# Seven block products instead of eight in the first half of the odd batches, and a new order of the sums they need

## The chip, the cores and the metric

The kernel runs on one core of a Trainium2 chip. The metric is the device time of one execution in microseconds (us), as a median over runs. All arithmetic of the matrix products is in 32-bit floats. The engines are TensorE (PE, with its weight loads shown as PEld), the vector engine (DVE), ScalarE (ACT), GpSimd (POOL) and SyncE (SP, which issues DMAs).

## The reference

A cross attention between 512 tokens and 32 state rows for each of 8 batches and 8 heads, and behind it a two-layer block with the activation h · cos(h). Cut to what matters:

```python
# x: (8, 8, 512, 64), state: (8, 8, 32, 64)
scores  = softmax(scale * x @ state.T)       # 512 x 32 for each head
xread   = scores @ state                     # 512 x 64
scores2 = softmax(scale * state @ x.T)
sread   = scores2 @ x                        # 32 x 64
rows = concatenate([xread, sread])           # 544 rows for each batch, 512 wide over the heads
h = rows @ w_in                              # 512 -> 2048, the first layer
g = h * cos(h)
out = g @ w_out                              # 2048 -> 512, the second layer
```

## The kernel before

**Stages.** Batch b has 16 tiles f of 128 hidden columns for its 512 tokens; the state rows of all batches are 16 more tiles at the end. The loop at the bottom takes one tile a step, 144 steps, and s is the step within a batch. It emits all engines' instructions in the order in which each engine is to run them: nothing reorders them later, and each engine runs its own list in order.

**The first layer.** The attention's second product is folded into the first layer: `sw` is the state times `w_in` (`products`, `products_kept`), `aT` the normalised attention weights, and h = sw · aT with an inner dimension of 256, in two pieces of 128. A plain tile (`hidden`) is two products of 128 x 128 weights with 512 columns, each of which shows as two instructions in the profile (a 32-bit product is made in two parts).

**Strassen's products.** `seven(t)` names the tiles whose first layer is made otherwise: two neighbouring tiles, t and t2, are a 2 x 2 block matrix (weights b11, b12, b21, b22) times the two halves of the tokens, and are made with seven products of 256 columns in place of eight. Before, these are the tiles of batches 2, 4 and 6 (`t.phase` is b % 2 * 2 + f // 8, so phases 0 and 1 are an even batch, 2 and 3 the two halves of an odd one). This needs:

- `halves(b)`: four differences of halves of aT into `aS`, on the vector engine, once a batch. For an even batch it stands five steps ahead. For a batch that follows a `seven` batch it would stand at s = 14; before, that place was never reached.
- `sw_sums(t)`: t1, t2, t4 in `swS` and a new b21 in place, four 128 x 128 operations for each pair, on Pool. For the first pair of an even batch it is emitted three steps ahead (just before `gate4`), for all others two steps ahead, at the end of the step, behind `blocks`.
- `hidden_a`: four of the products, one step ahead of the pair, into two PSUM tiles; a ScalarE copy; and `sums_a`, three additions on the vector engine.
- `hidden_b`: the other three products in the pair's own first step; `sums_b`, two additions. The tile pool of h has two PSUM tiles, and `hidden_a` and `hidden_b` take both, so each needs the sums of the other done.

**The activation.** `gate` (ScalarE, a rounding), `gate2` (vector, a difference), `gate3` (ScalarE, the sine) and `gate4` (vector, the product with h) make g = h · cos(h) in a slot of `g_all`. For a plain tile h is read in PSUM; for a `seven` tile it lies in `g_all` already.

**The second layer** uses seven block products too, over a pair of batches (`Pair`, `sums`, `sums2`, `p7`, `p4`, `output`). It needs differences of the tiles of both batches: `minus`, which runs on the vector engine when `soon` is true and the pair isn't the first, else on Pool. In phase 2 this is b0 = t - b0 for each tile; in phase 3 there are three. `output` multiplies a tile three steps after it was made (`LAG`). In phases 0 to 2 it also emits up to one left-over product of the pair before. `blocks` makes sums of blocks of w_out on Pool, at steps 16 to 22, 32 and 33.

**Order within a step** (the loop): `hidden_b` with its sums (and `halves` at s = 14), or `hidden`; `hidden_a` for the next pair; `gate`, `gate2`, `sums_a`, parts of the next batch's attention, `gate3`, one deferred store, the early `sw_sums`, `gate4`, `sums`, more parts, `halves`, `blocks`, the late `sw_sums`, `sums2`, and last `output` of the tile three steps back. Step 29 is tile 13 of batch 1, step 32 the first tile of batch 2.

Of the kernel before, what the change touches and what calls it, by code (L numbers as in the profile page):

```python
# [21 lines left out]
def kernel(  # L22
# [8 lines left out]
    nc = tc.nc  # L31
# [151 lines left out]
    def fetch(n):  # L183
        nonlocal n_fetched
        while n_fetched < n:
            dst, src = loads[n_fetched]
            if f64:
                m, w = dst.shape[1:]

                at_, c0 = (n_fetched - 2) % 3, 0  # L190
                if n_fetched < 4:
                    at_, c0 = n_fetched // 2, n_fetched % 2 * 2 * m * w
                if n_fetched >= N_LOADS:
                    at_ = 3 + n_fetched - N_LOADS
                raw = raw_at[at_].bitcast(I32)[:, c0:c0 + 2 * m * w]
                raw = raw.rearrange("p (m f) -> p m f", m=m)
                nc.sync.dma_start(out=raw, in_=src.bitcast(I32))
                raws[n_fetched] = raw.rearrange("p m (f w) -> p m f w", w=2)
            else:
                nc.sync.dma_start(out=dst, in_=src)  # L200
            n_fetched += 1
# [49 lines left out]
    class Attention:  # L251
# [126 lines left out]
        def sums(self):  # L378
            self.reduce1([self.z1[:, j] for j in range(2)], ALU.add)
            self.inverse(self.m1 if self.b == 0 else self.i12)  # L380
# [72 lines left out]
    def part(b, name, *args):  # L453

        if b not in attn:
            attn[b] = Attention(b)
        getattr(attn[b], name)(*args)
        if (name, args) == ("reads", (1,)) and b + 1 < B:
            if b > 0:
                attn[b + 1] = Attention(b + 1)  # L460
                attn[b + 1].load_tokens()
            load_x(b + 1)
# [5 lines left out]
    def hidden(t):  # L468
        t.hp = hps.tile([P, S], F32, name="h")[:, 0:t.n]
        for i in range(t.kn):  # L470
            nc.tensor.matmul(out=t.hp, lhsT=t.lhs(i), rhs=t.rhs(i),  # L471
                             start=(i == 0), stop=(i == t.kn - 1))
# [4 lines left out]


    def seven(t):
        return t.pair is not None and t.b > 1 and t.phase < 2  # L480

    def new_pair(t):
        return t.b % 2 == 0 and t.f == 0
# [9 lines left out]
    def blocks_of(t):  # L495
        sw = sw_of[t.b, P * t.f // WC]
        c = P * t.f % WC
        return [sw[:, j, c + P * r:c + P * r + P] for r in range(2)
                for j in range(2)]

    def sw_sums(t):
        b11, b12, b21, b22 = blocks_of(t)
        t1, t2, t4 = [swS[:, i] for i in range(3)]
        sub = ALU.subtract
        for o, x1, x2, op in ((t1, b21, b22, ALU.add), (t2, t1, b11, sub),
                              (t4, b12, t2, sub), (b21, b11, b21, sub)):
            nc.gpsimd.tensor_tensor(o, x1, x2, op=op)  # L507

    LO, HI = slice(0, HS), slice(HS, S)

# [36 lines left out]
    def hidden_b(t):  # L547
        b11, b12, b21, b22 = blocks_of(t)
        t.h1, t.h2 = [hps.tile([P, S], F32, name="h") for _ in range(2)]
        product_of(t.h1[:, LO], b12, aT_of[t.b][:, 1, LO])  # L550
        product_of(t.h2[:, HI], swS[:, 2], aT_of[t.b][:, 1, HI])
        product_of(t.h2[:, LO], b22, aS[:, 3])
# [29 lines left out]
    def minus(pr, out, a, b, soon=False):  # L582
        engine = nc.vector if soon and pr.n else nc.gpsimd
        engine.tensor_tensor(out, a, b, op=ALU.subtract)  # L584
# [78 lines left out]
    def sums(t):  # L663
        pr, i = t.pair, t.i
        pr.b[t.phase, i] = t
        if t.phase == 2:
            minus(pr, pr.b[0, i].g, t.g, pr.b[0, i].g, True)
        if t.phase == 3:
            minus(pr, pr.b[0, i].g, t.g, pr.b[0, i].g, True)
            minus(pr, pr.b[2, i].g, t.g, pr.b[2, i].g)  # L670
# [99 lines left out]
    def tiles():  # L770
        pr = None
        for b in range(B):
            if b % 2 == 0:
                pr = Pair(b // 2, pr)
            for f in range(NF):
                t = Tile()
                t.b, t.f, t.pair = b, f, pr
                t.phase, t.i = b % 2 * 2 + f // NH, f % NH
                t.n, t.kn = S, 2
                c = slice(P * f % WC, P * f % WC + P)  # L780
                t.lhs = lambda i, b=b, nt=P * f // WC, c=c: (
                    sw_of[b, nt][:, i, c])
                t.rhs = lambda i, b=b: aT_of[b][:, i]
                yield t
        for n in range(NF):
            t = Tile()
            t.b, t.n_th, t.f = B, n, (n + NH) % NF
            t.pair, t.last_pair, t.phase = None, pr, None
            t.n, t.kn = B * Ns, NK
            cols = slice(P * t.f, P * t.f + P)  # L790
            t.lhs = lambda i, cols=cols: w_in[:, i, cols]
            t.rhs = lambda i: sT[:, :, Ns * i:Ns * i + Ns]
            yield t


    def warm(n, to):

        for _ in range(n):
            nc.tensor.matmul(out=to, lhsT=zeros[:, 0:P], rhs=zeros, start=True,  # L799
                             stop=True)  # L800
# [123 lines left out]
    all_tiles = list(tiles())  # L924
    for step, t in enumerate(all_tiles):
        s = step % NF
        if s == 0 and t.b < B:
            steps = plan(t.b)
        todo = [p[s] if t.b < B else [] for p in steps]

        def go(n):
            for p in todo[n]:
                part(*p)

        last, conv = conv_at.get(step - 1, -1), conv_at.get(step, -1)
        if step == B * NF + (0 if f64 else 8):
            fetch(N_LOADS + 2)
        if step == 4:
            warm(1, acc[MAIN][0])
        ahead = all_tiles[step + 1:step + 3]  # L940
        if seven(t):
            if t.f % 2 == 0:
                hidden_b(t)
                sums_b(t)
                if s == NF - 2 and seven(all_tiles[step + 2]):
                    halves(t.b + 1)
        elif step != 1:
            hidden(t)
        first = len(ahead) > 1 and seven(ahead[0]) and ahead[0].f % 2 == 0
        if first:  # L950
            if not seven(t):

                h = t.hp
                take_slot(t)
                nc.scalar.copy(t.g, h)
            hidden_a(*ahead)
        if step == 0:
            hidden(all_tiles[1])
            warm(3, acc[MAIN][0])
            gate(t)  # L960
            gate2(t)
            convert(3, "bcdf")
            convert(4, "1")
            go(0)
        else:
            go(0)
            if step == 5:
                states(1, acc[SIDE][1])
            if not (seven(t) and t.f % 2):
                gate(t)  # L970
            gate2(t)
            if step == 3:
                warm(4, acc[MAIN][0])
                part(0, "products", 1, SIDE)
            if first:
                sums_a(ahead[0])
            go(1)
            go(3)
            if step == 1:
                convert(4, "bcdf")  # L980
            elif last >= 0:
                convert(last, "bcdf")
            if conv >= 0 and not todo[1]:
                convert(conv, "1")
        gate3(t)
        if seven(t) and t.f % 2 == 0:
            gate(t.second)
        if step == 3:
            part(0, "products_kept", 1, SIDE)
        if later:  # L990
            later.pop(0)()
        for u in all_tiles[step + 3:step + 4]:
            if seven(u) and new_pair(u):
                sw_sums(u)
        gate4(t)
        if conv >= 0 and todo[1] and step > 0:
            convert(conv, "1")
        if t.pair is not None:
            sums(t)
        if step == 6:  # L1000
            states_kept(1, acc[SIDE][1])
        go(2)
        if conv >= 0:
            convert(conv, "2")
        go(4)
        for u in all_tiles[step + 5:step + 6]:
            if seven(u) and new_pair(u):
                halves(u.b)
        if step in block_at:
            blocks(*block_at[step])  # L1010
        for u in all_tiles[step + 2:step + 3]:
            if seven(u) and u.f % 2 == 0 and not new_pair(u):
                sw_sums(u)
        if t.pair is not None:
            sums2(t)
        while len(line) >= (LAG if step >= 2 * NH else LAG + 1):
            output(line.pop(0))
        line.append(t)
# [32 lines left out]
```

## Time and profile before

| what | value |
|---|---|
| median of 5 runs | 769.31 us (768.81 to 770.35) |
| the profiled execution | 769.34 us, of which the span from first to last instruction is 767.5 us |
| granted TensorE clock | 1.000 |
| second layer, L622, 128x512 | 896 instructions, 413.6 us busy, 598 ns each |
| first layer, plain, L471, 128x512 | 320 instructions, 150.8 us busy, 594 ns each |
| first layer, seven products, L512, 128x256 | 336 instructions, 100.9 us busy, about 380 ns each |
| subtractions of tiles, L584 | 80 on Pool (1435 ns), 48 on the vector engine (697 ns) |
| block sums, L507 | 96 on Pool, 453 to 985 ns |
| DMA | 43.52 MB, 57 GB/s over the span |

How to read it: TensorE's instructions overlap, so the sum of their busy times is more than the time that they take; their spacing is read from the starts in the timeline. A row of a timeline has the start and the duration in us, the engine, the line of the kernel, the operation, the tile written and the tiles read, their shapes, how many such instructions follow each other, and in brackets the idle time ahead of it with what ended it. Short waits of TensorE behind a start can hide in the modelled end of the instruction before.

### The profile page before, as it was taken

Reading aid. Unit: us, or ns where it says so; the run is one execution under the profiler, and the core shown is the slowest. Engines: PE = TensorE matmul, PEld = TensorE weight load, DVE = VectorE, ACT = ScalarE, POOL = GpSimd, SP = SyncE. Lnnn points to the kernel's source line nnn. Section 1 sums busy time; section 2 is a strip of 40 time slices with the busy share of each in tenths; the row PEclk is TensorE's granted clock in tenths of the full one; section 3 lists DMA queues with packets and bytes.
Section 4 is the critical chain, followed back from the end, with each engine's and each line's share of the span. In section 5 each row is a group of like instructions: output and inputs, shape, how many; then the busy total and the mean of one; then the engine's idle time right before and its main releaser. Section 6 shows DMA issues by size and latency. Waiting matters only on the chain.

```text
span 767.5 us, 8094 instructions
## 1 busy us (share of the span) xinstructions
PE 755.7 (98%) x2808; PEld 366.9 (48%) x2808; DVE 487.3 (63%) x786; ACT 314.1 (41%) x511; POOL 227.8 (30%) x214
## 2 busy tenths in 40 slices
PE   8998999999999999999999999999999999999997
PEld 4443443444555434445555434455554444455554
DVE  5778787836896558847886558748876546432431
ACT  3877944532254325333362335333443333212112
POOL 2344278876120000653220001751210006500200
PEclk9999999999999999999999999999999999999999
DMA  9596471050002510340105211420100115000021
GB/s 246 168 273 198 137 104 28 8 102 1 12 16 47 91 28 2 54 83 0 29 0 100 39 27 16 76 46 0 28 1 14 23 20 138 0 1 14 15 41 41
DMA packets 161960, 43.52 MB, mean 57 GB/s; under 512 B 153920, under 2 KB 153920, under 8 KB 161920
## 3 DMA queue, kind: packets, MB, share of 16 engines
q1 hardware_dynamic: 161024, 42.49, 25.8%
q10 hardware_dynamic: 768, 0.39, 0.2%
q8 instruction: 22, 0.36, 0.2%
q0 software_dynamic: 128, 0.13, 0.1%
q14 instruction: 18, 0.15, 0.1%
HBM read 34.08 MB, written 8.91 MB: 56 GB/s over the span
## 4 chain that ended last, share of the span: by engine, by line
PE 91%; DVE 3%; POOL 2%; ACT 2%; DMA 1%; issue 1%; SPq 0%; DVEq 0%; POOLq 0%; ACTq 0%
PE o L622 49%; PE h L471 20%; PE h L512 9%; PE at L319 4%; PE o L742 4%; PE at L409 2%; PE o L319 1%; POOL g_all L584 1%; PE at L392 1%; DMA g_all<-in_moe_w_in_dram 1%; POOL w_out L910 0%; DVE q L568 0%; ACT q L565 0%; PE o L799 0%; DMA s<-in_state_dram 0%
## 5 line engine op out<-in xcount | busy, mean ns | idle before, releaser
L622 PE MATMUL o<-g_all,w_out 128*128 128x512 f32 x512 | 236.3, 598 | 0.4 <-POOL w_out L242 0.4
L584 POOL TENSOR_TENSOR g_all<-g_all 128x512 f32<-128x512 f32 x80 | 112.9, 1435 | 240.4 <-DVE g_all L578 240.4
L622 PE MATMUL o<-g_all,s 128*128 128x512 f32 x384 | 177.3, 598 | 0.0
L471 PE MATMUL h<-aT,sw 128*128 128x512 f32 x320 | 150.8, 594 | 2.9 <-DVE g_all L578 2.4
L568 DVE TENSOR_TENSOR q<-q,h 128x512 f32<-128x512 int32 (+1 forms) x93 | 59.4, 638 | 147.6 <-ACT q L565 147.6
L622 PEld LDWEIGHTS o<-g_all,w_out 128*128 128x128 f32 x512 | 93.8, 190 | 118.4 <-issue 114.6
L571 ACT ACTIVATE q<-q,halfpi 128x512 f32<-128x512 f32 (+1 forms) x144 | 100.9, 701 | 87.6 <-DVE q L568 87.5
L565 ACT ACTIVATE q<-h 128x512 int32<-128x512 f32 (+1 forms) x93 | 52.2, 562 | 201.1 <-PE h L471 200.9
L622 PEld LDWEIGHTS o<-g_all,s 128*128 128x128 f32 x384 | 70.8, 190 | 88.6 <-issue 86.6
L471 PEld LDWEIGHTS h<-aT,sw 128*128 128x128 f32 x320 | 60.1, 190 | 79.9 <-issue 66.5
L578 DVE TENSOR_TENSOR g_all<-h,q 128x512 f32<-128x512 f32 (+1 forms) x93 | 59.2, 637 | 35.0 <-ACT q L571 34.6
L565 ACT ACTIVATE q<-g_all 128x512 int32<-128x512 f32 x51 | 31.8, 623 | 90.9 <-DVE g_all L558 90.5
L568 DVE TENSOR_TENSOR q<-q,g_all 128x512 f32<-128x512 int32 x51 | 36.5, 716 | 28.6 <-ACT q L565 28.6
L242 POOL TENSOR_TENSOR w_out<-w_out,s 128x1024 int32<-128x1024 int32 x10 | 23.9, 2393 | 77.6 <-DVE w_out L237 62.8
L578 DVE TENSOR_TENSOR g_all<-g_all,q 128x512 f32<-128x512 f32 x51 | 37.0, 726 | 10.5 <-ACT q L571 10.4
L507 POOL TENSOR_TENSOR swS<-sw 128x128 f32<-128x128 f32 x24 | 11.4, 476 | 84.0 <-PE h L512 66.1
L584 DVE TENSOR_TENSOR g_all<-g_all 128x512 f32<-128x512 f32 x48 | 33.5, 697 | 1.6
L445 ACT COPY sw<-at 128x512 f32<-128x512 f32 x50 | 26.7, 586 | 10.4 <-PE at L319 10.0
L242 POOL TENSOR_TENSOR w_in<-w_in,s 128x1024 int32<-128x1024 int32 (+1 forms) x10 | 19.3, 1931 | 37.3 <-DVE w_in L237 22.0
L471 PE MATMUL h<-st_all,w_in 128*128 128x256 f32 x128 | 30.2, 379 | 0.0
L512 PE MATMUL h<-aS,swS 128*128 128x256 f32 x96 | 28.7, 380 | 1.0 <-POOL swS L507 1.0
L742 PE MATMUL o<-w_out,g_all 128*128 128x512 f32 x64 | 29.6, 592 | 0.0
(103 smaller groups left out, 788.2 us busy)
## 6 DMA issues: line engine op xcount, KB each, us to landing
out_dram<-ot SPq DMA_DIRECT2D x132, 64.0 KB, 2.0
g_all<-in_moe_w_out_dram SPq DMA_DIRECT2D x8, 1024.0 KB, 5.1
g_all<-in_moe_w_in_dram SPq DMA_DIRECT2D x6, 1024.0 KB, 5.3
xT<-in_x_dram SPq DMA_DIRECT2D x96, 64.0 KB, 2.5
x_b<-in_x_dram SPq DMA_DIRECT2D x24, 256.0 KB, 4.6
x_b<-in_x_dram SPq DMA_DIRECT2D x16, 128.0 KB, 4.2
g_all<-in_moe_w_in_dram SPq DMA_DIRECT2D x4, 512.0 KB, 6.2
x_b<-in_moe_w_out_dram SPq DMA_DIRECT2D x1, 1024.0 KB, 5.9
```

Of the source, the lines that this page charges most:

```text
L242: nc.gpsimd.tensor_tensor(bits, bits, e, op=ALU.add)
L319: nc.tensor.matmul(out=(to or at)[j][Ns * k:Ns * k + Ns, 0:n], lhsT=w[D * j:D * j + D, self.b, Ns * k:Ns * k + Ns], rhs=r(slice(D * j, D * ...
L445: (copy or nc.scalar.copy)(sw_of[self.b, nt][:, j, c0:c1], to[j][:, 0:c1 - c0])
L471: nc.tensor.matmul(out=t.hp, lhsT=t.lhs(i), rhs=t.rhs(i), start=(i == 0), stop=(i == t.kn - 1))
L512: nc.tensor.matmul(out=out, lhsT=w, rhs=r, start=True, stop=True)
L565: nc.scalar.activation(t.q.bitcast(I32), t.hp, func=ACTF.Copy, bias=0.25)
L568: nc.vector.tensor_tensor(t.q, t.q.bitcast(I32), t.hp, op=ALU.subtract)
L571: nc.scalar.activation(t.q, t.q, func=ACTF.Sin, bias=halfpi, scale=-TWO_PI)
L578: nc.vector.tensor_tensor(t.g, t.hp, t.q, op=ALU.mult)
L584: engine.tensor_tensor(out, a, b, op=ALU.subtract)
L622: nc.tensor.matmul(out=acc[bank][ch], lhsT=w[:, i, P * ch:P * ch + P], rhs=g.g, start=(i == 0), stop=(i == NH - 1))
L742: nc.tensor.matmul(out=acc[MAIN][i], lhsT=t.g[:, P * i:P * i + P], rhs=w_out[:, :, t.f, :], start=(t.n_th == 0), stop=(t.n_th == NF - 1))
```

## The change

Four edits:

1. `seven` covers phase 2 as well: tiles 0 to 7 of batches 3, 5 and 7. With it the branch at s = 14 of batches 2, 4 and 6 runs `halves` for the odd batch that follows.
2. `sw_sums` chooses its engine: the vector engine for the first pair of batch 2, Pool for all others.
3. The subtraction b0 = t - b0 of phase 2 goes from the vector engine to Pool in all pairs of batches (in the first pair it was there already).
4. The call of `sw_sums` two steps ahead moves from the end of the step, behind `blocks`, to just before `gate4`, where the three-steps-ahead call stood; both are now one loop.

```diff
     def seven(t):
-        return t.pair is not None and t.b > 1 and t.phase < 2
+        return t.pair is not None and t.b > 1 and t.phase < 3
...
         sub = ALU.subtract
+
+        engine = nc.vector if t.b < 2 or t.b == 2 and t.f == 0 else nc.gpsimd
         for o, x1, x2, op in ((t1, b21, b22, ALU.add), (t2, t1, b11, sub),
                               (t4, b12, t2, sub), (b21, b11, b21, sub)):
-            nc.gpsimd.tensor_tensor(o, x1, x2, op=op)
+            engine.tensor_tensor(o, x1, x2, op=op)
...
         if t.phase == 2:
-            minus(pr, pr.b[0, i].g, t.g, pr.b[0, i].g, True)
+            minus(pr, pr.b[0, i].g, t.g, pr.b[0, i].g)
...
-        for u in all_tiles[step + 3:step + 4]:
-            if seven(u) and new_pair(u):
+        for u, new in zip(all_tiles[step + 2:step + 4], (False, True)):
+            if seven(u) and u.f % 2 == 0 and new_pair(u) == new:
                 sw_sums(u)
         gate4(t)
...
         if step in block_at:
             blocks(*block_at[step])
-        for u in all_tiles[step + 2:step + 3]:
-            if seven(u) and u.f % 2 == 0 and not new_pair(u):
-                sw_sums(u)
```

## The prediction

> **What bounds the kernel now.** I read the page's busy line first, then busy time by window for the first halves of the batches, then the timeline of TensorE, and last those of Pool and the vector engine where TensorE stood still.
>
> ```profile
> PE 755.7 (98%) x2808; PEld 366.9 (48%) x2808; DVE 487.3 (63%) x786; ACT 314.1 (41%) x511; POOL 227.8 (30%) x214
> ```
>
> A busy TensorE could still be a slow one, so the windows come next: first half of batch 3 (plain products), then all of batch 4 (seven products).
>
> ```profile
> 254.60:296.00 41.40, 41.40 (x138) 17.13 (x137) 25.46 (x39) 12.38 (x21) 0.00 (x0) 1.00 0.20 32
> 338.10:422.30 84.20, 84.20 (x352) 45.97 (x351) 62.53 (x108) 34.98 (x61) 18.68 (x31) 1.00 0.17 30
> ```
>
> Columns: window, its length, then busy time and instructions of TensorE, weight loads, vector engine, ScalarE, Pool; then the granted clock. TensorE is busy for the whole of both windows at clock 1.00. In batch 3's first half Pool does nothing and the vector engine works 25.46 of 41.40 us, 61%; in batch 4 it works 62.53 of 84.20, 74%, and TensorE still doesn't wait. So the order of TensorE's own instructions sets the time, and an instruction taken from it is worth its spacing.
>
> Those spacings are in TensorE's timeline. Batch 3, one tile's plain products and what follows:
>
> ```profile
> 262.82 1.88 PE L471 MATMUL h<-aT,sw 128*128 128x512 f32 x4
> 264.54 3.60 PE L622 MATMUL o<-g_all,w_out 128*128 128x512 f32 x8
> ```
>
> Batch 4, the four products of `hidden_a` and the three of `hidden_b`:
>
> ```profile
> 349.37 0.59 PE L512 MATMUL h<-aT,sw 128*128 128x256 f32 x2
> ...
> 351.10 3.60 PE L622 MATMUL o<-g_all,s 128*128 128x512 f32 x8
> 354.53 0.59 PE L512 MATMUL h<-aT,sw 128*128 128x256 f32 x2
> ...
> 355.82 3.60 PE L622 MATMUL o<-g_all,s 128*128 128x512 f32 x8
> ```
>
> The starts count, since each modelled end overlaps the next start. A plain tile takes 264.54 - 262.82 = 1.72 us, a pair 3.44. The seven products take (351.10 - 349.37) + (355.82 - 354.53) = 1.73 + 1.29 = 3.02.
>
> **Part 1, seven products for 24 more tiles.** Batches 3, 5, 7, tiles 0 to 7: 12 pairs. TensorE loses 12 x (3.44 - 3.02) = 5.04 us. Upper bound: a whole product each, two instructions 0.215 apart, 12 x 0.43 = 5.2. Lower bound: in batches 2, 4 and 6 the timeline shows the second product of `hidden_b` late by some 0.19 at step 4 (batch 2: 197.00, then 197.55 where 0.43 is usual, and 0.08 more inside it); if the three new batches have it too, 5.04 - 0.6 = 4.4. I take 5.04: that delay follows four bank evacuations on the vector engine (2.44 us from 192.76), and the first half of an odd batch has two.
>
> It adds for each pair one ScalarE copy (0.37) and five vector sums of 0.41, 0.42, 0.69, 0.42, 0.69 = 2.63 us. The subtraction b0 = t - b0 (0.69 a tile) leaves the vector engine. Per batch: 4 x 2.63 - 8 x 0.69 = +5.0 us, so the half window goes to about 30.5 us in 39.7, 77%: the load of batch 4. What hides it: between one `hidden_a` and the next `hidden_b` lie 3.43 us of output products. In batch 4 `hidden_a` ends at 351.10, the last of its sums at 352.54, and `hidden_b` starts at 354.53: 2.0 us of cover. Without that cover each late us would be TensorE's.
>
> `halves` now also runs at step 14 of batches 2, 4, 6: 4 x 0.41 = 1.6 us on the vector engine, after sums that end at 252.08 in batch 2, so till 253.7. `hidden_a` of the odd batch starts where a small transpose does now, 254.63, and needs them from its second product on, 0.43 later, 255.06. Queued behind it is the second gate step of tile 14, which goes from 252.84 to about 253.7; its tile is multiplied three steps later. Cost 0, cover 1.4 us. No DMA is moved, and neither SP's nor ScalarE's queue is passed.
>
> **Part 2, Pool's new work and the order of its queue.** The 24 subtractions cost Pool 1.27 to 1.44 each, 30 to 35 us; 12 more sets of block sums 4 x 0.46 = 1.84 each, less one set that goes to the vector engine. In a stretch of 41.4 us where Pool is idle a batch gets 8 x 1.44 + 4 x 1.84 = 18.9. The subtraction waits for `gate4`, its result is read three steps later (some 15 us), so it costs TensorE nothing. Only the sets have a date: two operations before, two after `hidden_b`, all before the next `hidden_a`. In batch 4 they end at 356.58 for a product at 359.69.
>
> The danger is what Pool does to the vector engine. Vector engine, then Pool, at step 11 of batch 3:
>
> ```profile
> 318.70 1.49 DVE L493 TENSOR_TENSOR aS<-aT 128x256 f32<-128x256 f32 x1
> 320.22 1.38 DVE L493 TENSOR_TENSOR aS<-aT,aS 128x256 f32<-128x256 f32 x1
> 321.52 0.41 DVE L493 TENSOR_TENSOR aS<-aT 128x256 f32<-128x256 f32 x1
> 318.14 3.19 POOL L584 TENSOR_TENSOR g_all<-g_all 128x512 f32<-128x512 f32 x2 [0.39 <-DVE g_all L578]
> ```
>
> While Pool's two subtractions run, an operation of 0.41 takes 1.49 and 1.38; when they are over it takes 0.41. The price is up to 1.08 us per Pool subtraction, for vector operations with both inputs in SBUF: `gate2` and `gate4` of these tiles. The sums into g_all read one input from PSUM, and I see none stretched so. One subtraction falls in each step, so `gate2` can be 1.1 us late, against 2.0 us of cover: price 0 on TensorE, upper bound below as a rival.
>
> The Trainium skill ("SBUF — State Buffer", section "Who interferes with whom") speaks against this edit: a vector instruction with two SBUF inputs and a GpSimd instruction that reads SBUF lock each other out for the whole instruction, so work goes to Pool at the vector engine's cost. The rows agree on the hold. Were each hold paid on TensorE, the sum would end 24 x 1.08 = 26 us higher, near 788; by the cover in the rows it stays.
>
> The block sums now stand ahead of `blocks` and of the subtractions. Where Pool was behind, this pays. TensorE, then Pool, at steps 31 to 33:
>
> ```profile
> 180.14 0.59 PE L512 MATMUL h<-aT,sw 128*128 128x256 f32 x2
> 181.76 0.70 PE L512 MATMUL h<-aS,swS 128*128 128x256 f32 x2 [1.02 <-POOL swS L507]
> ...
> 183.67 3.60 PE L622 MATMUL o<-g_all,s 128*128 128x512 f32 x8
> 173.43 3.73 POOL L584 TENSOR_TENSOR g_all<-g_all 128x512 f32<-128x512 f32 x3 [3.23 <-DVE g_all L578]
> 177.11 2.87 POOL L910 TENSOR_TENSOR w_out<-w_out 128x1024 f32<-128x1024 f32 x1
> 179.94 0.91 POOL L507 TENSOR_TENSOR swS<-sw 128x128 f32<-128x128 f32 x1
> ```
>
> This `hidden_a` took 183.67 - 180.14 = 3.53 us for 1.73: 1.80 lost, since its sums stood behind the L910 block. After the change they start at 177.1 and end at 177.1 + 4 x 0.46 = 179.0, at worst (0.91 each) 180.8; the second product wants two of them at 180.57, the third the last one at 181.0. Gain 1.80, at worst about 1.6. L910, late by 2 to 3 us, is used from 193.56 on. It may now hold `gate2` of step 33, with the sums of `hidden_a` queued behind: held over all of it, to 179.0 + 2.87 = 181.9, gate and sums end near 184.2, and `hidden_b` starts at 180.14 + 1.73 + 3.43 = 185.3.
>
> **Part 3, one set on the vector engine.** The set for batch 2, tile 0 leaves Pool (159.35 to 161.3) at step 29. A 128x128 addition on the vector engine is not in the trace: from below the 32x128 row, 0.285; from above the 128x256 row, 0.41, or 1.49 if Pool holds each one. I take 0.285, the row of the same length: 1.14 us from 159.27, when ScalarE's copy lands, to 160.4. Pool is idle from 158.6 until `gate4`, so the hold should not occur; with it, 159.27 + 4 x 1.49 = 165.2, still ahead of the use at 168.88. Behind it waits `gate4` of step 29 (160.00 before, 160.4 now), and behind that Pool's three subtractions, which began at 161.25 after the set and can now begin at 161.1. Cost 0, gain 0. TensorE's delay of 0.40 + 0.07 at 169.1 waits for a ScalarE copy, which stays; were it to go, 0.5.
>
> **The sum.** -5.04 - 1.80 = -6.84. The profiled execution took 769.34 (span 767.5 and 1.8 around it), next to a median of 769.31: 769.34 - 6.84 = **762.5 us**. Bounds of the costs: 769.34 - 5.2 - 1.8 - 0.5 = 761.8, and 769.34 - 4.4 - 1.6 = 763.3.
>
> **Rivals.**
> - *Part of it is paid back* (0.17): `halves` at step 14 is held by Pool's sums as at 318.70, 4 x 1.08 more, ending at 258.0 instead of 253.7, past 255.06; or the set at step 32 stays late. For it: the rows of 1.49. Against: Pool's operations there are of 0.46, not 1.4. With two of the four held (2.2 us) it ends at 255.9, 0.8 late in three batches: 762.5 + 2.4 = 764.9; with the step 32 delay kept instead, 764.3.
> - *Pool's lock becomes the bound: slower* (0.10). Place: `gate2` ahead of the sums of `hidden_a`, in the 12 odd steps. If the subtraction and a block sum both hold it, the cover of 2.0 us is gone, and the following hold of 1.49 is paid by TensorE: 12 x 1.49 = 17.9, so 762.5 + 17.9 = 780.4. It decides from 6.84 / 12 = 0.57 us a pair. Against: the second half of batch 3 has two Pool subtractions a step and a TensorE that is busy throughout; there, though, no step needs both h buffers.
> - *The products don't get cheaper* (0.04): with 128x256 pieces the weight load (190 ns) nearly fills the spacing (215 ns), and another wait at the seams of plain and seven eats the rest; 768 to 769.5. Against: the 3.02 us of a pair is measured with those weight loads in it.
>
> **Numbers.** Forecast 0.69; its own range 761.8 to 763.3. With part paid back the range reaches 766. The runs before span 1.5 us, so 0.2% (1.5 us) is what a measurement of this kernel tells from no change. Faster: 0.69 + 0.17 = 0.86; within: 0.04; slower: 0.10.
>
> **What will show it.** Right: 36 sets at the line of the block sums, four of these operations on the vector engine; 12 x 14 more short products and 48 x 2 fewer long ones; no wait inside the `hidden_a` of step 33; TensorE busy throughout the odd first halves, each 1.7 us shorter. Wrong: TensorE waiting for g_all's sums in an odd first half, with `gate2` rows of 1.5 us before them; or `hidden_a` of step 15 waiting for aS.

## The result, and the profile after

The changed kernel takes 767.92 us (median of 25 runs, 766.29 to 770.05) against 769.92 of the kernel before (47 runs): the ratio is 0.9974, with a 95% interval of 0.9967 to 0.998. It is faster, by 2.0 us; 6.8 were forecast, and the time lies above the range. The profiled execution took 766.71 us, with a span of 764.9.

The start of the kernel, ahead of everything that changed, varies by some tenths of a microsecond to some microseconds from run to run. So spans are compared below from the first product of the first `hidden_a` (168.45 us before, 167.82 after) to the end: 767.53 - 168.45 = 599.08 before, 764.92 - 167.82 = 597.10 after, 1.98 less.

Page of the changed kernel, busy time and the chain that ended last:

```profile
PE 750.4 (98%) x2880; PEld 379.9 (50%) x2880; DVE 515.0 (67%) x838; ACT 316.2 (41%) x523; POOL 275.9 (36%) x282
PE 86%; DVE 8%; ACT 3%; issue 1%; DMA 1%; POOL 1%; SPq 0%; DVEq 0%; ACTq 0%; POOLq 0%
```

TensorE's busy time fell by 5.3 us, the span by 2.6, and the vector engine's share of the chain is 8% where it was 3%: a new wait, on that engine. TensorE's waits by cause show it (engine, line, what it waited for, total us, times, longest):

```profile
PE h L471 <- DVE g_all L580: 4.7, 4, 1.9
PE o L624 <- DVE held L637: 1.4, 2, 0.7
```

The first was 2.4 in two waits before, the second is new, and the wait for Pool's block sums (1.0) is gone. TensorE's timeline has the new waits at step 11 of batch 3 (and in the same places of batch 5):

```profile
306.12 1.88 PE L624 MATMUL o<-g_all,s 128*128 128x512 f32 x4
309.19 1.98 PE L471 MATMUL h<-aT,sw 128*128 128x512 f32 x4 [1.19 <-DVE g_all L580]
...
312.13 2.84 PE L624 MATMUL o<-g_all,s 128*128 128x512 f32 x6
315.66 1.12 PE L624 MATMUL o<-g_all,s 128*128 128x512 f32 x2 [0.69 <-DVE held L637]
```

By starts, 309.19 is 1.35 late (306.12 + 1.72 = 307.84) and 315.66 is 0.85 late. The first is `hidden` of step 11, which needs the h buffer that `gate4` of step 9 frees; the second is a product into a bank that the vector engine hasn't emptied. Behind each wait another 0.1 is lost where the next weights weren't loaded ahead (the rows of the weight loads start again only at 309.19 and 315.66): 2.4 us in each of batches 3 and 5, 4.8 in all. Forecast gain 6.84 less 4.8 leaves 2.0.

Why is the vector engine late? Its timeline, and Pool's, just ahead:

```profile
302.54 0.65 DVE L580 TENSOR_TENSOR g_all<-h,q 128x512 f32<-128x512 f32 x1
303.30 1.79 DVE L586 TENSOR_TENSOR g_all<-g_all 128x512 f32<-128x512 f32 x1
305.01 1.23 DVE L339 STREAM_TRANSPOSE xT<-i 128x1024 f32<-128x1024 f32 x1
...
303.27 1.27 POOL L586 TENSOR_TENSOR g_all<-g_all 128x512 f32<-128x512 f32 x1 [5.37 <-DVE g_all L580]
305.17 1.28 POOL L586 TENSOR_TENSOR g_all<-g_all 128x512 f32<-128x512 f32 x1 [0.63 <-DVE g_all L586]
```

The same place before:

```profile
305.73 0.65 DVE L578 TENSOR_TENSOR g_all<-h,q 128x512 f32<-128x512 f32 x1
306.42 0.69 DVE L584 TENSOR_TENSOR g_all<-g_all 128x512 f32<-128x512 f32 x1
...
306.46 3.00 POOL L584 TENSOR_TENSOR g_all<-g_all 128x512 f32<-128x512 f32 x2 [65.12 <-DVE g_all L578]
```

Both engines start a subtraction as soon as `gate4` is done: the vector engine b0 = t - b0 of phase 3, Pool b2 = t - b2. Before, the vector engine started 0.69 after its `gate4`, 0.04 ahead of Pool; it took 0.69, and Pool waited. Now it starts 0.76 after, 0.03 behind Pool, and takes 1.79. The view of that source line says what the 0.07 is. Changed kernel (operation, times; durations in ns, least/median/most; DVEq and POOLq are the instruction queues of the two engines):

```profile
L586 DVE TENSOR_TENSOR g_all<-g_all x24: 691/1065/1801, 303.3 to 667.6; 128x512 f32<-128x512 f32 x24
L586 POOLq EVENT_SEMAPHORE  x17: 17/17/5347, 104.3 to 172.8; - x17
L586 DVEq EVENT_SEMAPHORE  x12: 21/21/21, 303.2 to 648.1; - x12
```

There are twelve instructions on the vector engine's queue that only wait for a semaphore; before, that line had none of them. They belong to the first four subtractions of phase 3 in batches 3, 5 and 7, the ones held. The other twelve of the same line in the same run have no such instruction, and all take 0.69. The reason is edit 3: b0 is now last written by Pool, in phase 2, so the subtraction has Pool to wait for beside `gate4`. In the trace's record of the semaphores the subtraction now carries Pool's, and the extra instruction ahead of it carries the one of `gate4`. Pool's write was done long ago, but the extra instruction itself costs 0.07 us and with it the race.

### The profile page after: what moved, and what is told of

The parts are those of the page before. It is cut to its first block, busy times and chain, and to the rows that moved or that the text cites. A ratio compares the mean times of both kernels' runs of the same rounds, so it can differ in the third digit from the quotient of the medians.

```text
span 764.9 us, 8437 instructions
## 1 busy us (share of the span) xinstructions
PE 750.4 (98%) x2880; PEld 379.9 (50%) x2880; DVE 515.0 (67%) x838; ACT 316.2 (41%) x523; POOL 275.9 (36%) x282
## 4 chain that ended last, share of the span: by engine, by line
PE 86%; DVE 8%; ACT 3%; issue 1%; DMA 1%; POOL 1%; SPq 0%; DVEq 0%; ACTq 0%; POOLq 0%
PE o L624 47%; PE h L514 14%; PE h L471 13%; PE at L319 4%; PE o L744 4%; PE at L409 2%; DVE g_all L586 1%; PE o L319 1%; DVE q L570 1%; DVE xT L339 1%; DVE g_all L580 1%; DVE i L333 1%; ACT q L567 1%; PE at L392 1%; DVE aT L356 1%
## 5 line engine op out<-in xcount | busy, mean ns | idle before, releaser
L586 POOL TENSOR_TENSOR g_all<-g_all 128x512 f32<-128x512 f32 x104 | 140.6, 1365 | 142.9 <-DVE g_all L580 135.4
L471 PE MATMUL h<-aT,sw 128*128 128x512 f32 x224 | 105.9, 596 | 5.3 <-DVE g_all L580 4.7
L570 DVE TENSOR_TENSOR q<-q,h 128x512 f32<-128x512 int32 (+1 forms) x69 | 42.8, 620 | 98.5 <-ACT q L567 98.5
L567 ACT ACTIVATE q<-g_all 128x512 int32<-128x512 f32 x75 | 46.8, 624 | 144.9 <-DVE g_all L560 144.5
L570 DVE TENSOR_TENSOR q<-q,g_all 128x512 f32<-128x512 int32 x75 | 53.2, 710 | 35.5 <-ACT q L567 35.5
L580 DVE TENSOR_TENSOR g_all<-g_all,q 128x512 f32<-128x512 f32 x75 | 54.1, 722 | 14.2 <-ACT q L573 14.1
L580 DVE TENSOR_TENSOR g_all<-h,q 128x512 f32<-128x512 f32 (+1 forms) x69 | 42.8, 620 | 23.0 <-ACT q L573 22.5
L514 PE MATMUL h<-aS,sw 128*128 128x256 f32 x144 | 43.1, 381 | 0.1
L509 POOL TENSOR_TENSOR swS<-sw,swS 128x128 f32<-128x128 f32 x35 | 18.2, 521 | 68.7 <-PE h L514 67.8
L514 PE MATMUL h<-aT,sw 128*128 128x256 f32 x144 | 42.8, 379 | 0.0
```

Source lines behind the costliest of these rows:

```text
L471: nc.tensor.matmul(out=t.hp, lhsT=t.lhs(i), rhs=t.rhs(i), start=(i == 0), stop=(i == t.kn - 1))
L509: engine.tensor_tensor(o, x1, x2, op=op)
L514: nc.tensor.matmul(out=out, lhsT=w, rhs=r, start=True, stop=True)
L567: nc.scalar.activation(t.q.bitcast(I32), t.hp, func=ACTF.Copy, bias=0.25)
L570: nc.vector.tensor_tensor(t.q, t.q.bitcast(I32), t.hp, op=ALU.subtract)
L580: nc.vector.tensor_tensor(t.g, t.hp, t.q, op=ALU.mult)
```

## The experiments

The theory that these test: TensorE lost 4.8 us because the vector engine's subtractions in phase 3 lose a race against Pool by 0.07 us (**lock**). Its rival: the vector engine has too much to do behind the new sums, whoever comes first (**overload**).

The ratios are to runs of the kernel before that were made beside each experiment (their median is 769.74 for order_alone to pool_order, 769.49 from early_look on). The fourth column comes from one profiled execution of each.

| run | median us | ratio to before, 95% interval | first group to end | TensorE's waits at step 11 of batch 3 |
|---|---|---|---|---|
| changed kernel | 767.92 | 0.9974 (0.9967 to 0.998) | 597.10 | 1.35 + 0.85 |
| order_alone | 767.21 | 0.9974 (0.9963 to 0.9985) | 597.2 | none |
| minus_alone | 769.64 | 0.9999 (0.9991 to 1.0008) | 599.1 | none |
| minus_back | 764.96 | 0.9947 (0.9934 to 0.996) | 595.3 | 0.34 (step 10) + 0.96 |
| pool_order | 764.47 | 0.9938 (0.9926 to 0.995) | 593.9 | 1.06 |
| early_look | 764.79 | 0.9937 (0.9925 to 0.9949) | 594.2 | 0.83 |
| norm_late | 768.44 | 0.9989 (0.9979 to 0.9999) | 597.7 | 0.50 + 1.77 + 0.21 |
| order_and_norm | 762.11 | 0.9903 (0.989 to 0.9916) | 592.1 | 0.20 |
| look_and_norm | 764.57 | 0.9936 (0.9924 to 0.9948) | 594.6 | 1.17 |

**order_alone**: the changed kernel with edits 1 and 3 undone.

```diff
-        return t.pair is not None and t.b > 1 and t.phase < 3
+        return t.pair is not None and t.b > 1 and t.phase < 2
...
-            minus(pr, pr.b[0, i].g, t.g, pr.b[0, i].g)
+            minus(pr, pr.b[0, i].g, t.g, pr.b[0, i].g, True)
```

> The kernel before with the block sums' new place and engine alone. As predicted for this part: TensorE's wait of 1.80 us in the step 33 product group goes, nothing else moves, time 1.8 us below the kernel before. If the delay only moves to a later place in Pool's queue: within 0.5 us of the kernel before.

Measured: 1.9 us less from the first group to the end, 2.0 by the ratio and 2.5 between the medians. The `hidden_a` of step 33 runs without a gap. So the new order of the block sums is worth what was forecast, and it is all that the change as a whole brought: the seven products of the odd batches, with the subtraction on Pool, added 0.1 us (597.2 against 597.10).

**minus_alone**: the kernel before with edit 3 alone.

```diff
-            minus(pr, pr.b[0, i].g, t.g, pr.b[0, i].g, True)
+            minus(pr, pr.b[0, i].g, t.g, pr.b[0, i].g)
```

> The kernel before with the subtraction of phase 2 on Pool and nothing else. Lock theory: the first four subtractions of the vector engine in phase 3 of batches 3, 5 and 7 take 1.79 us instead of 0.69, TensorE waits at step 11 of batches 3 and 5 where it did not, time 1 to 4 us above the kernel before. Overload theory: the vector engine has 0.6 us less to do in 24 steps, no wait appears, time within 0.5 us of the kernel before.

Measured: no change, and no subtraction held. The lock theory's expectation was wrong, and the source view of the line says why:

```profile
L584 POOLq EVENT_SEMAPHORE  x42: 17/17/5347, 104.2 to 670.2; - x42
L584 DVE TENSOR_TENSOR g_all<-g_all x24: 691/692/739, 305.7 to 669.5; 128x512 f32<-128x512 f32 x24
L584 DVEq EVENT_SEMAPHORE  x12: 21/21/21, 305.7 to 648.9; - x12
```

The twelve waits are there on the vector engine, but Pool's queue has twelve more too (30 before): by the record of the semaphores its subtraction waits for Pool's own earlier one as well. In the changed kernel new block sums lie between the two, which is likely why that wait is missing there. The counts of the other runs fit, 32 in order_alone without these sums and 17 in minus_back with them; it was not tried by itself. Both start 0.07 later, the vector engine stays 0.04 ahead and is not held. So the run doesn't tell the theories apart; it shows that the wait alone does no harm as long as the other engine carries the same one.

**pool_order**: the changed kernel; Pool's b2 subtraction behind the one that needs the vector engine's result.

```diff
         if t.phase == 3:
             minus(pr, pr.b[0, i].g, t.g, pr.b[0, i].g, True)
-            minus(pr, pr.b[2, i].g, t.g, pr.b[2, i].g)
...
             minus(pr, pr.b[1, i].g, pr.b[1, i].g, pr.b[0, i].g)
+            minus(pr, pr.b[2, i].g, t.g, pr.b[2, i].g)
```

> The changed kernel with Pool's two subtractions of a step in the second half of an odd batch in the other order, so that the first of them waits for the vector engine's subtraction. Lock theory: all 24 subtractions of the vector engine there take 0.69 us; the wait for gate4 at step 11 falls from 1.35 to between 0.2 and 0.8 us and the bank wait from 0.85 to under 0.3 us in batches 3 and 5; time 2 to 4 us below the changed kernel. Overload theory: both waits stay within 0.3 us of what they are, time within 1 us of the changed kernel.

Measured: 3.2 us below the changed kernel from the first group on. No subtraction of the vector engine takes 1.79 any more (the longest takes 0.96), and the wait for the bank is gone. The wait for `gate4` is 1.06, not the 0.2 to 0.8 expected. What is left is in good part the same lock at another operation. The normalisation of the attention, ahead of `gate4` of step 9, meets Pool's second subtraction:

```profile
306.33 2.01 DVE L386 TENSOR_TENSOR aT<-aT,xT 128x1024 f32<-128x1024 f32 x1
304.76 2.51 POOL L586 TENSOR_TENSOR g_all<-g_all 128x512 f32<-128x512 f32 x2 [6.17 <-DVE g_all L586]
```

It takes 2.01 here, 1.80 in early_look and minus_back, and 1.79 in the kernel before, where TensorE still had slack; in the changed kernel it took 1.20.

Of the 3.2 us, 2.5 fall at step 11 of batches 3 and 5. Nearly all of the rest falls in step 10 of batches 2, 4 and 6, 0.23 in each: there the second product of `hidden_b` is late in the changed kernel, as it was before, and not in pool_order. The rows of batch 2 show another race, between `gate2` and a block sum on Pool. Changed kernel:

```profile
222.41 0.46 POOL L509 TENSOR_TENSOR swS<-sw 128x128 f32<-128x128 f32 x1 [5.02 <-ACT sw L445]
222.48 0.94 DVE L570 TENSOR_TENSOR q<-q,g_all 128x512 f32<-128x512 int32 x1
```

pool_order:

```profile
223.33 1.00 POOL L509 TENSOR_TENSOR swS<-sw 128x128 f32<-128x128 f32 x1 [5.05 <-ACT sw L445]
223.36 0.65 DVE L570 TENSOR_TENSOR q<-q,g_all 128x512 f32<-128x512 int32 x1
```

Why this one is won in pool_order is not shown; in early_look and minus_back it is lost as before.

**minus_back**: the changed kernel with edit 3 undone.

```diff
-            minus(pr, pr.b[0, i].g, t.g, pr.b[0, i].g)
+            minus(pr, pr.b[0, i].g, t.g, pr.b[0, i].g, True)
```

> The changed kernel with the subtraction of phase 2 back on the vector engine. Lock theory (in the second half of an odd batch the vector engine's subtraction now starts 25 ns after Pool's instead of 44 ns ahead, because it has a semaphore of Pool to wait for, and is held 1.1 us): all 24 subtractions there are back at 0.69 us, lead 44 ns, and TensorE's two waits of step 11 (1.35 and 0.85 us in batches 3 and 5) get shorter though the vector engine has 0.6 us more to do in each tile of the first half; time 1 to 4 us below the changed kernel. Overload theory (the vector engine has simply too much to do from step 5 on): the waits grow by up to 1.8 us a batch, time 1 to 4 us above the changed kernel.

Measured: 1.8 us below the changed kernel from the first group on, although the vector engine has 0.69 more to do in each of 24 tiles; its phase 3 subtractions take 0.69 to 0.70, but for two of 0.80 and 0.81, as before. Overload alone would have made it slower. The waits of 0.34 and 0.96 that remain are longer together than in pool_order (1.06): there the extra work probably shows.

**early_look**: the changed kernel with one small instruction added ahead of `gate4`; Pool's queue stays as it is. `seen` is a column that nothing else reads.

```diff
+        if t.phase == 3 and t.i == 0 and t.pair.n:
+            nc.vector.tensor_copy(seen, t.pair.b[0, NH - 1].g[:, 0:1])
         gate4(t)
```

> The changed kernel with one copy of a single column on the vector engine ahead of gate4 at step 8 of batches 3, 5 and 7; it waits for Pool's last subtraction of the first half, so the twelve subtractions behind it no longer have a semaphore of Pool to wait for. Pool's own queue is as in the changed kernel. If the 70 ns of that wait decide the race: the twelve go from 1.79 to 0.69 us, start 44 ns ahead of Pool's again, TensorE's waits at step 11 of batches 3 and 5 fall from 1.35 and 0.85 to 0.7 to 1.1 and under 0.1 us, and the time is within 1 us of pool_order's 764.5. If it was Pool's order or load that held them: 1.79 us stays, time as the changed kernel, 767 to 768.5.

Measured: 2.9 us below the changed kernel from the first group on. This is the cleanest of the tests: no work is taken away or moved, one copy is added, and the source view has no waiting instruction on the vector engine's queue left:

```profile
L587 DVE TENSOR_TENSOR g_all<-g_all x24: 691/692/811, 304.7 to 666.1; 128x512 f32<-128x512 f32 x24
L587 POOLq EVENT_SEMAPHORE  x17: 17/17/5337, 104.9 to 174.3; - x17
```

The copy takes that wait once, where it costs 0.11 us of the vector engine. The race is won again by 0.04:

```profile
304.03 0.67 DVE L581 TENSOR_TENSOR g_all<-h,q 128x512 f32<-128x512 f32 x1
304.74 0.69 DVE L587 TENSOR_TENSOR g_all<-g_all 128x512 f32<-128x512 f32 x1
...
304.79 3.01 POOL L587 TENSOR_TENSOR g_all<-g_all 128x512 f32<-128x512 f32 x2 [5.43 <-DVE g_all L581]
```

The wait left, 0.83, is shorter than in pool_order (1.06) by about as much as the normalisation is held less, 1.80 against 2.01.

**norm_late**: the changed kernel; the normalisation of the attention moves behind `gate4` of its step.

```diff
-            x_dve[s[6]].append((b, "norm1"))
+            y_dve[s[6]].append((b, "norm1"))
```

> The changed kernel with the normalisation (1.2 us on the vector engine, 2.0 when held) behind gate4 in its step instead of ahead of it. Queue theory for what pool_order left (the vector engine's list ahead of gate4 of step 9 is longer than TensorE's shortened steps 6 to 10): the wait for gate4 at step 11 falls from 1.35 to under 0.3 us; the holds stay, so the wait for the bank stays at 0.8 to 2.1 us; time 0 to 3 us below the changed kernel. If that list is not the cause: 1.35 stays.

Measured: 0.6 us above the changed kernel from the first group on. The wait for `gate4` fell to 0.50, not under 0.3, but a new one of 1.77 came:

```profile
PE at L409 <- ACT xT L397: 3.4, 2, 1.7
PE h L471 <- DVE g_all L580: 3.0, 4, 1.9
```

The ScalarE copy L397 overwrites rows that the normalisation reads, so it waits for it, and TensorE's products of step 11 wait for the copy. With the subtraction ahead of it still held for 1.79, the normalisation came too late: it ran at 313.31, for a product that could have started at 313.4. I hadn't counted that reader.

**order_and_norm**: pool_order and norm_late together.

> pool_order and norm_late together: both waits of step 11 under 0.3 us, the full 5.0 us of the products and the 1.8 us of the new order reach the end; time 2 to 3 us below pool_order, 761.5 to 762.5 us. If the second cause is in TensorE's or ScalarE's queue: 764.5 as pool_order.

Measured: 762.11 us, 7.0 less than before from the first group on: the forecast for the change itself was 762.5. With nothing held, the normalisation fits behind `gate4`:

```profile
306.56 0.69 DVE L580 TENSOR_TENSOR g_all<-h,q 128x512 f32<-128x512 f32 x1 [0.17 <-ACT q L573]
307.36 0.69 DVE L586 TENSOR_TENSOR g_all<-g_all 128x512 f32<-128x512 f32 x1
307.96 1.22 DVE L386 TENSOR_TENSOR aT<-aT,xT 128x1024 f32<-128x1024 f32 x1
```

and TensorE's `hidden` of step 11 starts without a gap, at 307.89. One wait of 0.20 in each of batches 3 and 5 is left, for the ScalarE copy. That the total meets the forecast is in part luck: the 0.4 us of these waits are made up by step 10 of batches 2 and 6, where the race of `gate2` is won as in pool_order, 0.23 each, which the forecast didn't have in it. This is the fastest version of the study.

**look_and_norm**: early_look and norm_late together.

> early_look and norm_late together: as order_and_norm within 0.8 us, since the two ways of keeping the vector engine ahead of Pool should be worth the same.

Measured: 764.57, 2.5 us above order_and_norm, where 0.8 was allowed for. The two remedies are not worth the same. Here Pool's two subtractions follow at once on the vector engine's own, and the normalisation behind it runs into them:

```profile
306.95 0.69 DVE L587 TENSOR_TENSOR g_all<-g_all 128x512 f32<-128x512 f32 x1
307.56 2.29 DVE L387 TENSOR_TENSOR aT<-aT,xT 128x1024 f32<-128x1024 f32 x1
```

2.29 us for 1.22, and TensorE waits 1.17 for the ScalarE copy behind it. In order_and_norm Pool has to be told first that the vector engine's subtraction is done; in that time the normalisation starts, and it is Pool that waits.

## Why the prediction was wrong

- **The products (part 1): right.** From `hidden_a` at s = 15 to `hidden` of step 8, batch 3 takes 295.45 - 252.14 = 43.31 us; before it was 299.59 - 254.63 = 44.96. That is 1.65 a batch, 5.0 in three, as forecast. No wait of TensorE falls in any of the three first halves.
- **`halves` at step 14: right.** Four operations from 249.51 to 251.06, none held; the second product of `hidden_a` came at 252.57. The partial rival built on them did not happen.
- **The order of the block sums (part 2): right in kind and size.** `hidden_a` of step 33 took 1.73; its sums started at 176.61, right behind the subtractions.

```profile
179.45 0.59 PE L514 MATMUL h<-aT,sw 128*128 128x256 f32 x2
179.88 0.59 PE L514 MATMUL h<-aS,swS 128*128 128x256 f32 x2
...
176.61 0.91 POOL L509 TENSOR_TENSOR swS<-sw 128x128 f32<-128x128 f32 x1
179.82 4.67 POOL L912 TENSOR_TENSOR w_out<-w_out 128x1024 f32<-128x1024 f32 x2
```

- **The set on the vector engine (part 3): right.** Four operations of 0.28 to 0.29, from 158.68 to 159.83, 1.15 us for the 1.14 taken.
- **The step that failed: "The subtraction waits for `gate4`, its result is read three steps later (some 15 us), so it costs TensorE nothing."** The next reader of b0 is not TensorE alone. In phase 3 the vector engine subtracts from the same tile, and an edit that moves the writer to another engine gives that reader a semaphore to wait for. I counted what Pool's new work would do to `gate2` and `gate4` in the first half, and found cover; the harm came eight steps later, in a line that the change doesn't touch, from a second wait, on something long done, and it cost TensorE 2.4 us in each of batches 3 and 5. The hold itself, 1.1 us for one Pool subtraction, was priced rightly and put in the wrong half.
- **The evidence I took for cover said the opposite.** I argued that the second half of batch 3 has two Pool subtractions a step and a busy TensorE. It has, but with hardly any slack: before, `gate4` of step 9 ended at 311.10 + 0.65 = 311.75, and the `hidden` that needs its buffer started at 311.98. I read how full TensorE was and not how far behind it the vector engine ended.
- **What the shorter first half does to the second was left out.** TensorE reaches step 11 earlier by 1.65 us, and the vector engine's list does not get shorter by as much: from `hidden_a` to the end of `gate4` of step 9 it takes 311.75 - 254.63 = 57.12 us before and 308.89 + 0.65 - 252.82 = 56.72 in pool_order. That leaves a wait of 1.06 there, with no subtraction ahead of it held, and the wait goes when the normalisation leaves the place ahead of `gate4` (order_and_norm). But Pool's hold has the larger part of it too: without the 0.81 by which the normalisation is held, an estimate, 0.25 of the 1.06 would be left, and 0.23 of early_look's 0.83 without 0.60. So both theories have a share, and overload the small one, about a quarter of a microsecond in each of two batches. In first-group-to-end time, winning the race at step 11 is worth 2.5 us in pool_order and 2.9 in early_look; moving the normalisation on top of pool_order is worth another 1.75; moving it alone costs 0.6.
- **Batch 7 is the control in the same run.** Its first four subtractions are held too (635.50, 1.80 us), and TensorE does not wait: no attention follows it, and the vector engine has room. Here the hold costs time only where that list is full.
- **The rivals.** The slower one had the mechanism, Pool holding the vector engine, at the wrong place, and expected it to be paid in every odd step; it was paid in one place in each of two batches. That the products don't get cheaper is refuted by the 1.65.

The Trainium skill's rule on this ("SBUF — State Buffer", section "Who interferes with whom") also says that the order of issue decides who blocks. The rows agree: starts 0.04 ahead and 0.03 behind are 0.69 and 1.79 us for the same operation.

What stays open: what would take away the last 0.20 in order_and_norm wasn't tried, and why pool_order wins the race at step 10 of the even batches isn't known.

## What to carry to other kernels

When an operation moves to another engine, list every later reader of what it writes: each one on the old engine can get a second semaphore to wait for, even if the value has long been there, and with it an instruction of its own. Here twelve of 24 readers got one, and it cost 0.07 us each on the engine's list. Where two engines start on the same signal and exclude each other, that decides who goes first; make the order explicit, by a dependence of the one that has time. And before shortening the bound engine's work, measure in the stages that follow how late the second engine already ends, not how busy the first one is.

## What the runs showed of the hardware that was not expected

A lead of some tens of nanoseconds is stable: in all twelve places of the changed kernel the vector engine lost, in ten of the twelve of early_look it won by 0.04 us, and in the other two Pool was still busy with an earlier subtraction (0.81 us, as in the kernel before). The times of the held operation agree within some 20 ns, except one that Pool had entered 0.38 us earlier (1.44 us instead of 1.79). The sign of the recorded lead is not the whole of it: at step 10 of the even batches Pool's block sum is held (1.00 us) where its start is recorded 37 to 46 ns ahead of that of `gate2` (three places in pool_order, two in order_and_norm), and goes through (0.46) where it is 53 to 78 ns ahead (the third place in order_and_norm, and all three in every other run). An instruction that only waits for a semaphore shows as 21 ns on the queue, but moved the start of the next operation by 70 ns.
